# A fused retention and feed-forward kernel on one NeuronCore: FF units grouped by four for the weight loads, and alpha loaded straight into its place

## The chip, the core and the metric

The kernel runs on one core of a Trainium2 chip. The metric is the time of one execution on the device in microseconds (us), smaller being better. The times of the kernel before are 307.03, 307.56 and 306.79 us: a median of 307.03 us. The profiled execution, from which all rows of the trace come, took 306.96 us itself.

## What is computed

Two layers stand behind each other. The first is a retention layer (attention without a softmax, with a decay that depends on the distance of two positions) for 8 batches, 8 heads, 576 positions and 64 elements per head. The second is a feed-forward (FF) layer on the 4608 tokens that come out, with 512 inputs, 2048 FF units and a "snake" activation.

```python
scores = scale * (q @ k.T)                     # per batch and head
ret = scores * Dmat                            # gamma[h] ** (i - j) for i >= j, else 0
x = (ret @ v)                                  # 4608 x 512 after joining the heads
h = x @ w_in                                   # 4608 x 2048
s = sin(alpha * h)                             # alpha: one number for each FF unit
g = h + s * s / (alpha + 1e-9)
out = g @ w_out                                # 4608 x 512
```

Everything comes in and goes out as 32-bit floats (f32); the products are made from 16-bit floats (f16). The FF units may be numbered in any order inside the kernel, if the columns of w_in, the entries of alpha and the rows of w_out all follow the same order.

## The kernel before

**FF layer.** The 4608 tokens are nine blocks of 512. For a block n and a group fc of 128 FF units, `project(n, fc)` (L516) makes four matmuls at L524, one for each 128 rows of w_in: the stationary operand (the weights, loaded by a weight load of its own) is a 128 x 128 piece of w_in, the moving operand 512 token columns of `xT`. Some calls are split in two halves of 256 columns. `sine` (L529) on ScalarE makes sin(alpha h) from the PSUM result with alpha as a scale for each partition, `square` (L537) squares it on ScalarE, VectorE or GpSimd, and `product` (L546) on VectorE puts h + s s / alpha into `gT`. `gemm2(n, u)` (L562) then multiplies: 128 tokens of gT are the weights, a row group of w_out (128 x 512) the moving operand, 16 row groups summed for each 128 tokens; `finish` (L556) copies the sum to SBUF and stores it.

**Retention layer.** `load` (L110) fetches q, k and v of one batch and one half of the positions with one DMA of 512 KB on SyncE's queue; `cast` (L133) scales them to f16 on GpSimd (`G_`), VectorE (`V`) or ScalarE (`A_`); `turn` (L196) transposes them on TensorE and `take` (L209) copies the result out of PSUM (from batch 2 on, `crossed` transposes with a DMA instead). `outer`, `scores`, `masked`, `values`, `add_states` and `keep` then make the tokens' `xT`.

**Order of work.** The order is written out by hand, call after call, from L629 on: each engine executes its own calls in the order of the text. Up to L1113 the first three token blocks are interleaved with the first batches; from L1115 on a loop does the rest by a fixed plan. So an engine that waits for something holds back all that stands behind it on that engine, and TensorE's order is the same in every run.

**Loads of the weights.** w_in and w_out are loaded by GpSimd's DMA queue, which casts f32 to f16 under way, in four quarters each: `load_w_in(g)` (L90) fetches 512 columns of all four row groups, `load_w_out(g)` (L94) fetches 512 rows. In both, what is contiguous in DRAM is 512 f32, 2 KB: each DMA of 1 MB of f32 consists of 512 such runs. They stand in GpSimd's order at L656, L659, L678, L688 (w_in, quarters 0, 2, 1, 3) and L690, L727, L737, L773 (w_out, quarters 0 to 3). SyncE's queue meanwhile loads q, k and v in the order L637 to L799, among them batch 1's k for its two halves (L759, L763) and v for its second half (L799). Their consumers are the casts of k on GpSimd (L760 and L783), the turns on TensorE behind them (L764 and L800), and the cast of v on ScalarE (L807, L808) with `outer` behind it (L809).

**alpha.** alpha is loaded by ScalarE's queue as 16 partitions of 128 contiguous numbers (`alpha_r`, L631), transposed by a small matmul against a 16 x 16 identity that stands in the constants (`turn_alpha`, L582, called at L667), and copied to `alpha_t`, 128 partitions of 16 numbers (`take_alpha`, L586, L668). Column fc of `alpha_t` holds the alphas of the FF units 128 fc to 128 fc + 127.

Of the kernel before, what the change touches and what calls it, by code (L numbers as in the profile page):

```python
# [10 lines left out]
F32 = mybir.dt.float32  # L11
F16 = mybir.dt.float16
# [5 lines left out]
def kernel(  # L18
# [13 lines left out]

    nc = tc.nc

    B, H, S, D = q.shape
    DM, FF = moe_w_in.shape
    NT = out.shape[0]
    P = 128  # L40
    assert (H, S, D) == (8, 576, 64) and H * D == DM and B * S == NT
    FC = FF // P
    KT = DM // P
# [6 lines left out]
    cn_np = np.zeros((P, 84), dtype=np.float64)  # L50
# [6 lines left out]
        cn_np[:, 40 + h] = scale * gamma[h] ** (ii - 64)  # L57
    for a in range(4):
        cn_np[:, 48 + a] = gamma[4 * hi + a] ** 128
    cn_np[0:16, 68:84] = np.eye(16)  # L60

    cn_dram = nc.inline_tensor(cn_np.astype(np.float32), name="rt_cn")

    const = ctx.enter_context(tc.tile_pool(name="c", bufs=1))
    work = ctx.enter_context(tc.tile_pool(name="w", bufs=1))
    psum = ctx.enter_context(tc.tile_pool(name="p", bufs=1, space=bass.MemoryType.PSUM))
# [4 lines left out]
    cn = const.tile([P, 84], F32, tag="cn", bufs=1)  # L71
    fac = {"k": cn[:, 0:16], "q": cn[:, 16:32], "halved k": cn[:, 52:68]}
    fac_s = {"k": cn[:, 32:40], "q": cn[:, 40:48]}
    g1 = cn[:, 48:52]
    eye = cn[0:16, 68:84]
    alpha_r = const.tile([FC, P], F32, tag="alpha_r", bufs=1)
    alpha_t = const.tile([P, FC], F32, tag="alpha", bufs=1)
    inva = const.tile([P, FC], F32, tag="inva", bufs=1)
    w_in16 = const.tile([P, KT, FF], F16, tag="w_in16", bufs=1)
    w_out16 = const.tile([P, FC, 512], F16, tag="w_out16", bufs=1)  # L80
    sS = const.tile([P, B, 4, D], F16, tag="sS", bufs=1)
    xS = const.tile([P, KT, 512], F16, tag="xS", bufs=1)

    src = {"q": q, "k": k, "v": v}
    w_in_r = moe_w_in.rearrange("(a p) f -> p a f", p=P)
    w_out_r = moe_w_out.rearrange("(a p) d -> p a d", p=P)

    V, A_, G_ = nc.vector, nc.scalar, nc.gpsimd

    def load_w_in(g):  # L90
        cols = slice(g * 512, (g + 1) * 512)
        nc.gpsimd.dma_start(w_in16[:, :, cols], w_in_r[:, :, cols])  # L92

    def load_w_out(g):  # L94
        nc.gpsimd.dma_start(w_out16[:, 4 * g : 4 * g + 4, :], w_out_r[:, 4 * g : 4 * g + 4, :])

    def halves(n):
        return slice(64 * n, 64 * n + 64)
# [118 lines left out]
    matmul = nc.tensor.matmul  # L217
# [287 lines left out]
    xs = {8: xS}  # L505
    gT = {}
    hps_of = {}
# [3 lines left out]
    def bank(tag):  # L511
        if tag[0] == "m":
            return psum.tile([P, 2, 512], F32, tag=tag, bufs=1, name="hps")[:, 0]
        return psum.tile([P, 512], F32, tag=tag, bufs=1, name="hps")

    def project(n, fc, tag, part=None):  # L516

        if n not in gT:
            gT[n] = work.tile([P, FC, 512], F16, tag="gT", bufs=2, name="gT")
        if (n, fc) not in hps_of:  # L520
            hps_of[n, fc] = [bank(tag), None]
        cols = PART[part]
        for a in range(KT):
            matmul(  # L524
                hps_of[n, fc][0][:, cols], w_in16[:, a, fc * P : (fc + 1) * P], xs[n][:, a, cols],
                start=(a == 0 and part != 1), stop=(a == KT - 1), skip_group_check=True,
            )

# [46 lines left out]
    held = {}  # L575

    def keep_busy(n, tag, m=512):
        idle = psum.tile([P, 512], F32, tag=tag, bufs=1, name="idle")
        for _ in range(n):
            matmul(idle[:, 0:m], zero[:, 0:P], zero[:, 0:m], start=True, stop=True)  # L580

    def turn_alpha():  # L582
        held["al"] = psum.tile([P, FC], F32, tag="op", bufs=1, name="al_ps")
        matmul(held["al"], alpha_r, eye, start=True, stop=True, is_transpose=True)

    def take_alpha():  # L586
        nc.scalar.copy(alpha_t, held["al"])

    def invert_alpha():
        nc.vector.tensor_scalar_add(inva, alpha_t, 1e-9)  # L590
        nc.vector.reciprocal(inva, inva)
# [5 lines left out]
    def make_constants():  # L597

        ge = mybir.AluOpType.is_ge
        nc.gpsimd.memset(ident, 0.0)  # L600
        nc.gpsimd.affine_select(
            out=ident, in_=ident, compare_op=mybir.AluOpType.not_equal, fill=1.0,
            base=0, pattern=[[-1, P]], channel_multiplier=1,
        )
        nc.gpsimd.memset(mask, 1.0)
        for g in range(2):
            m = mask[halves(g), 0:256].rearrange("p (r g i) -> p r g i", r=2, g=2)
            nc.gpsimd.affine_select(
                out=m, in_=m, compare_op=ge, fill=0.0,
                base=0, pattern=[[-1, 2], [1, 2], [2, 64]], channel_multiplier=-2,  # L610
            )
            m = mask[halves(g), 256:320]
            nc.gpsimd.affine_select(
                out=m, in_=m, compare_op=ge, fill=0.0, base=0, pattern=[[1, 64]], channel_multiplier=-1,
            )
# [12 lines left out]
    with tc.manual_schedule():  # L628
        nc.scalar.dma_start(cn, cn_dram.ap())  # L629
        make_constants()  # L630
        nc.scalar.dma_start(alpha_r, moe_alpha.rearrange("(a p) -> a p", p=P))  # L631
        first = work.tile([P, 1], F32, tag="first", bufs=1, name="first")
        nc.vector.memset(first, 0.0)
        nc.scalar.activation(first, first, mybir.ActivationFunctionType.Sin)
# [19 lines left out]
        load(0, "q", 1)  # L654
        cast(0, "q", 1, G_)
        load_w_in(0)  # L656
        load(0, "k", 1)
        cast(0, "k", 1, V)
        load_w_in(2)  # L659
        turn(0, "q", 1, "h0")  # L660
        at[0].scores(0, 1, "m0")
# [2 lines left out]
        take(0, "k", 1, A_)  # L664
        load(0, "v", 1)
        at[0].scores(0, 0, "m1")
        turn_alpha()  # L667
        take_alpha()  # L668
        keep_busy(10, "h2", 256)
        take(0, "q", 1, A_)  # L670
        load(1, "q", 1)
# [4 lines left out]
        at[0].masked(0, 1)  # L676
        at[0].masked(0, 0)
        load_w_in(1)  # L678
        at[0].outer((1,), "h2", "h1")
        cast(1, "q", 1, G_)  # L680
# [7 lines left out]
        load_w_in(3)  # L688
        at[0].to_state(2, G_)
        load_w_out(0)  # L690
        at[0].values(0, False, "m0")
        at[0].values(0, True)
# [5 lines left out]
        at[0].add_states(1)  # L698
        at[0].keep(0, V)
        project(0, 2, "m1", 0)  # L700
        at[0].keep(1, V, A_)
        project(0, 2, "m1", 1)
        sine(0, 2)
        project(0, 1, "op")
        keep_busy(2, "h0")
        square(0, 2, V)
# [18 lines left out]
        product(0, 3)  # L725
        project(0, 11, "m1")
        load_w_out(1)  # L727
        sine(0, 8)
        turn(1, "q", 0, "op")
# [5 lines left out]
        square(0, 6, V)  # L735
        at[0].to_state(3, G_)
        load_w_out(2)  # L737
        square(0, 11, A_)
        product(0, 6)
# [456 lines left out]
        for c in range(3):  # L1196
            tag = next(h)
# [3 lines left out]
        for cols, eng in ((slice(0, 320), A_), (slice(320, 512), V)):  # L1201
            tag = next(h)
# [33 lines left out]
```

## Time and profile before

| what | value |
|---|---|
| time, median of 3 runs | 307.03 us (306.79 to 307.56) |
| the profiled execution's own time | 306.96 us |
| its span from the first to the last instruction | 305.2 us |
| TensorE's share of the span with a matmul under way | 96% |
| VectorE, ScalarE, GpSimd busy | 67%, 60%, 45% |
| bytes read from and written to DRAM | 36.75 MB and 9.44 MB |

The 1.8 us between the span and the time lie outside the first and the last instruction. "PE" is TensorE's matmuls, "PEld" its weight loads, "DVE" VectorE, "ACT" ScalarE, "POOL" GpSimd, "SPq" SyncE's DMA queue. A busy TensorE says only that a matmul was under way, not that it ran at its full rate. "L524" is line 524 of the kernel. In rows of instructions a number pair at the head is start and length in microseconds, "x16" is a count, and the bracket at the end is how long the engine stood idle before it and what ended the wait. In rows of DMA queues, q1 is SyncE's queue, q0 GpSimd's and q10 ScalarE's; the three numbers are packets, megabytes written, and the time that the packets took as a share of 16 DMA engines over the stretch (reads and writes overlap, so more than 100% is possible).

### The profile page before, as it was taken

To read this page: it belongs to the slowest core of one execution; us is meant where nothing else is said; L and a number is where in the kernel's file an instruction comes from. 1 tells how busy PE (TensorE), PEld (TensorE's weight loads), DVE (VectorE), ACT (ScalarE), POOL (GpSimd) and SP (SyncE) were. 2 spreads that over 40 slices of the span, in tenths; PEclk is the share of its full clock that TensorE was granted. 3 is DMA by queue.
4 is the path that set the end of the run, shared out by engine and by line. 5 is a ranking of instruction groups with operands and counts; after the bars stand their busy time and mean duration, and the time that the engine had idled before them with its cause. 6 is when DMAs were issued, how large, how long until landed. Compare 5 with 4: busy or idle time off the path is not lost.

```text
span 305.2 us, 7933 instructions
## 1 busy us (share of the span) xinstructions
PE 293.5 (96%) x3257; PEld 149.6 (49%) x3257; DVE 204.5 (67%) x296; ACT 182.7 (60%) x294; POOL 136.2 (45%) x155
## 2 busy tenths in 40 slices
PE   6879989999999999999999999999999999999995
PEld 5655556455444544454445444544454454444443
DVE  2768988899679796767665777566666746555600
ACT  1649935675365758665677567756764556555411
POOL 4794760498379488578039726653030000000000
PEclk9799999999999999999999999999999999999999
DMA  8999999997695978978689989866441111111132
GB/s 232 338 217 216 216 247 330 242 312 188 166 256 167 167 175 199 255 124 181 146 226 178 170 190 257 161 143 161 105 112 37 34 37 37 35 35 37 46 88 72
DMA packets 115508, 49.85 MB, mean 163 GB/s; under 512 B 69760, under 2 KB 110992, under 8 KB 115472
## 3 DMA queue, kind: packets, MB, share of 16 engines
q1 hardware_dynamic: 110912, 44.97, 62.8%
q0 software_dynamic: 4224, 4.19, 8.1%
q8 instruction: 25, 0.41, 0.6%
q10 hardware_dynamic: 336, 0.18, 0.3%
q14 instruction: 11, 0.09, 0.1%
HBM read 36.75 MB, written 9.44 MB: 151 GB/s over the span
## 4 chain that ended last, share of the span: by engine, by line
PE 82%; DMA 9%; POOL 3%; DVE 2%; ACT 1%; SPq 1%; issue 1%; DVEq 0%; ACTq 0%
PE ops L567 39%; PE hps L524 36%; DMA v<-in_v_dram 7%; PE sc L347 2%; PE o L389 2%; DMA q<-in_q_dram 2%; PE kv L283 1%; POOL q L169 1%; SPq L121 1%; POOL w_in L92 1%; PE o L411 1%; DVE ss_t L543 1%; DVE k L169 0%; DVE ret L359 0%; ACT v L102 0%
## 5 line engine op out<-in xcount | busy, mean ns | idle before, releaser
L567 PE MATMUL ops<-w_out,gT 128*128 128x512 f16 (+2 forms) x592 | 142.4, 373 | 0.9 <-DMA w_out<-in_moe_w_out_dram 0.4
L548 DVE SCALAR_TENSOR_TENSOR gT<-ss_t,inva,hps 128x512 f16<-128x512 f16 x144 | 106.2, 745 | 52.0 <-ACT ss_t L541 45.5
L532 ACT ACTIVATE s_t<-hps,alpha_t 128x512 f16<-128x512 f32 x144 | 97.3, 687 | 70.9 <-PE hps L524 68.1
L524 PE MATMUL hps<-xT,w_in 128*128 128x512 f16 (+1 forms) x544 | 126.5, 367 | 0.3
L524 PEld LDWEIGHTS <-w_in 128*128 128x128 f16 x608 | 58.6, 98 | 64.5 <-DVE xT L104 0.6
L567 PEld LDWEIGHTS <-gT 128*128 128x128 f16 x592 | 56.3, 98 | 65.0 <-issue 1.6
L543 DVE TENSOR_TENSOR ss_t<-s_t 128x512 f16<-128x512 f16 x72 | 43.6, 608 | 19.3 <-ACT s_t L532 18.7
L541 ACT ACTIVATE ss_t<-s_t 128x512 f16<-128x512 f16 x62 | 38.8, 632 | 0.9
L102 ACT COPY osb<-ops 128x512 f32<-128x512 f32 (+1 forms) x34 | 19.7, 582 | 22.0 <-PE ops L567 20.6
L169 POOL TENSOR_TENSOR k<-k,cn 128x1024 f16<-128x1024 f32 (+1 forms) x13 | 22.3, 1712 | 22.1 <-DMA k<-in_k_dram 17.9
L169 POOL TENSOR_TENSOR q<-q,cn 128x1024 f16<-128x1024 f32 (+1 forms) x16 | 27.2, 1710 | 10.9 <-DMA q<-in_q_dram 10.9
L359 DVE TENSOR_TENSOR ret<-sc,mask 128x1024 f16<-128x1024 f32 x20 | 23.9, 1219 | 4.2 <-PE sc L347 4.2
L329 POOL TENSOR_TENSOR kvs<-s,kvs 128x256 f32<-128x256 f32 x22 | 16.2, 734 | 4.0 <-ACT kvs L102 2.3
L543 POOL TENSOR_TENSOR ss_t<-s_t 128x512 f16<-128x512 f16 x10 | 10.8, 1084 | 14.6 <-ACT s_t L532 14.6
L102 ACT CAST xT<-o 128x1024 f16<-128x1024 f32 (+1 forms) x14 | 13.2, 957 | 6.1 <-PE o L411 5.9
L524 PE MATMUL hps<-xS,w_in 128*128 128x512 f16 x64 | 16.4, 379 | 0.0
L153 POOL TENSOR_TENSOR ks<-ks,cn 128x512 f16<-128x512 f32 x4 | 4.2, 1044 | 24.6 <-DMA vs<-in_v_dram 18.1
L104 POOL CAST v<-v 128x1024 f16<-128x1024 f32 (+1 forms) x10 | 10.0, 1007 | 11.1 <-DMA v<-in_v_dram 11.1
L328 POOL TENSOR_TENSOR s<-kvs,cn 128x256 f32<-128x256 f32 x22 | 14.3, 650 | 0.3
L321 POOL TENSOR_TENSOR s<-kvs,cn 128x256 f16<-128x256 f32 x19 | 12.2, 646 | 0.9 <-ACT kvs L102 0.4
L389 PE MATMUL o<-ret,v 64*64 64x128 f16 (+1 forms) x512 | 11.0, 214 | 0.9 <-DVE ret L359 0.4
L359 DVE TENSOR_TENSOR ret<-sc,mask_halved 128x768 f16<-128x768 f32 x12 | 11.4, 950 | 0.0
(62 smaller groups left out, 148.9 us busy)
## 6 DMA issues: line engine op xcount, KB each, us to landing
out_dram<-osb SPq DMA_DIRECT2D x70, 128.0 KB, 2.8
q<-in_q_dram SPq DMA_DIRECT2D x16, 512.0 KB, 5.4
k<-in_k_dram SPq DMA_DIRECT2D x10, 512.0 KB, 5.6
v<-in_v_dram SPq DMA_DIRECT2D x10, 512.0 KB, 6.4
k<-in_k_dram SPq DMA_DIRECT2D x24, 128.0 KB, 3.1
v<-in_v_dram SPq DMA_DIRECT2D x24, 128.0 KB, 3.3
w_in<-in_moe_w_in_dram POOLq DMA_DIRECT2D x4, 512.0 KB, 11.6
w_out<-in_moe_w_out_dram POOLq DMA_DIRECT2D x4, 512.0 KB, 11.5
```

Source lines behind the costliest of these rows:

```text
L102: eng.copy(d_, s_)
L169: eng.tensor_tensor(dst[:, a0:a1].rearrange("p a r t d -> p t (a r) d"), t_.rearrange("p (t a) x -> p t a x", t=2)[:, :, a0:a1].rearrange( ...
L328: nc.gpsimd.tensor_tensor(s32, self.kvs[:, c - 1], g1.unsqueeze(2).to_broadcast([P, 4, D]), MULT)
L329: nc.gpsimd.tensor_tensor(self.kvs[:, c], s32, self.kvs[:, c], ADD)
L359: nc.vector.tensor_tensor(ret.rearrange("p t (z x) -> p (t z) x", z=2)[:, :, 0:n], sc.rearrange("p t (z x) -> p (t z) x", z=2)[:, :, 0:n], ...
L389: made.append(matmul(o[t][halves(e), c : c + 128].rearrange("p (r i) -> p r i", r=2)[:, :, i0:64], v16[halves(g), 4 * t + 2 * x + e, r, :] ...
L524: matmul(hps_of[n, fc][0][:, cols], w_in16[:, a, fc * P : (fc + 1) * P], xs[n][:, a, cols], start=(a == 0 and part != 1), stop=(a == KT - ...
L532: nc.scalar.activation(s_t, hps, mybir.ActivationFunctionType.Sin, bias=0.0, scale=alpha_t[:, fc : fc + 1],)
L541: nc.scalar.activation(ss_t, s_t, mybir.ActivationFunctionType.Square)
L543: eng.tensor_tensor(ss_t, s_t, s_t, MULT)
L548: nc.vector.scalar_tensor_tensor(gT[n][:, fc, :], ss_t, inva[:, fc : fc + 1], hps, MULT, ADD)
L567: matmul(ops[n, c, cols.start][:, cols], gT[n][:, fk, c * P : (c + 1) * P], w_out16[:, fk, cols], start=(fk == 0), stop=(fk == FC - 1), sk ...
```

## The change

FF unit 512 g + 4 p + j now belongs to quarter g, partition p, place j. Its row of w_out goes to partition p of row group 4 g + j; so the four rows that one partition takes in a quarter lie behind one another in DRAM, one run of 8 KB, and a DMA of w_out consists of 128 runs, not 512. The columns of w_in are still loaded in their old order, in runs of 2 KB, now into four tiles, one for each quarter; `project` picks the 128 columns of a group with a step of 4 elements (8 bytes), so all weight loads at L524 read SBUF with that step. alpha is loaded directly into `alpha_t`: 128 partitions of four runs of four numbers (16 bytes) each, 512 runs; the matmul that transposed it, the copy behind it, the identity in the constants and the tile `alpha_r` are gone. The order of the instructions on each engine is the same otherwise. One wait moves: the matmul for alpha had waited for alpha's DMA, now the first `sine` and the first instruction of `invert_alpha` do.

```diff
-    alpha_r = const.tile([FC, P], F32, tag="alpha_r", bufs=1)
...
-    w_in16 = const.tile([P, KT, FF], F16, tag="w_in16", bufs=1)
+    w_in16 = [const.tile([P, KT, 512], F16, tag=f"w_in16_{g}", bufs=1, name=f"w_in16_{g}") for g in range(4)]
...
-    w_out_r = moe_w_out.rearrange("(a p) d -> p a d", p=P)
+    w_out_r = moe_w_out.rearrange("(g p j) d -> p g j d", p=P, j=4)
...
-        nc.gpsimd.dma_start(w_in16[:, :, cols], w_in_r[:, :, cols])
+        nc.gpsimd.dma_start(w_in16[g], w_in_r[:, :, cols])
...
-        nc.gpsimd.dma_start(w_out16[:, 4 * g : 4 * g + 4, :], w_out_r[:, 4 * g : 4 * g + 4, :])
+        nc.gpsimd.dma_start(w_out16[:, 4 * g : 4 * g + 4, :], w_out_r[:, g])
...
-                hps_of[n, fc][0][:, cols], w_in16[:, a, fc * P : (fc + 1) * P], xs[n][:, a, cols],
+                hps_of[n, fc][0][:, cols], w_in16[fc // 4][:, a, fc % 4 :: 4], xs[n][:, a, cols],
...
-    def turn_alpha():
-        held["al"] = psum.tile([P, FC], F32, tag="op", bufs=1, name="al_ps")
-        matmul(held["al"], alpha_r, eye, start=True, stop=True, is_transpose=True)
-
-    def take_alpha():
-        nc.scalar.copy(alpha_t, held["al"])
...
-        nc.scalar.dma_start(alpha_r, moe_alpha.rearrange("(a p) -> a p", p=P))
+        nc.scalar.dma_start(
+            alpha_t.rearrange("p (g j) -> p g j", j=4), moe_alpha.rearrange("(g p j) -> p g j", p=P, j=4)
+        )
...
-        turn_alpha()
-        take_alpha()
```

More of the change, by code (lines that the diff above doesn't have):

```diff
@@ L59 @@
         cn_np[:, 48 + a] = gamma[4 * hi + a] ** 128
-    cn_np[0:16, 68:84] = np.eye(16)
     cn_dram = nc.inline_tensor(cn_np.astype(np.float32), name="rt_cn")
@@ L74 @@
     g1 = cn[:, 48:52]
-    eye = cn[0:16, 68:84]
-    alpha_r = const.tile([FC, P], F32, tag="alpha_r", bufs=1)
     alpha_t = const.tile([P, FC], F32, tag="alpha", bufs=1)
     inva = const.tile([P, FC], F32, tag="inva", bufs=1)
-    w_in16 = const.tile([P, KT, FF], F16, tag="w_in16", bufs=1)
+    w_in16 = [const.tile([P, KT, 512], F16, tag=f"w_in16_{g}", bufs=1, name=f"w_in16_{g}") for g in range(4)]
     w_out16 = const.tile([P, FC, 512], F16, tag="w_out16", bufs=1)
```

## The prediction, as it was made before the changed kernel had run

> **What bounds the kernel now.** I read the page first (span, busy shares, chain by engine), then the chain in order of time, then the DMA queues and the engines in the stretch where the chain leaves TensorE.
>
> ```profile
> span 305.2 us, 7933 instructions
> ...
> PE 293.5 (96%) x3257; PEld 149.6 (49%) x3257; DVE 204.5 (67%) x296; ACT 182.7 (60%) x294; POOL 136.2 (45%) x155
> ...
> PE 82%; DMA 9%; POOL 3%; DVE 2%; ACT 1%; SPq 1%; issue 1%; DVEq 0%; ACTq 0%
> ```
>
> ```profile
> 3.35 5.95 DMA q<-in_q_dram
> ...
> 9.36 1.90 POOL q L169
> ...
> 11.26 1.58 POOL w_in L92 x2
> ```
>
> ```profile
> 20.57 22.89 DMA v<-in_v_dram
> ...
> 43.48 1.15 ACT v L102 x2
> ...
> 44.67 0.45 PE kv L283 x32
> ...
> 54.76 0.86 PE ops L567 x4
> 55.62 0.86 PE hps L524 x4
> ```
>
> From about 45 us TensorE is the chain: four matmuls of 512 columns take 0.86 us, 215 ns each, whether L524 or L567. Ahead of that the end hangs on loads: q's second half releases GpSimd at 9.36, which then issues w_in, and batch 1's second v, issued at 20.57, is consumed only at 43.48. So there are two questions: does the change make TensorE's steady 215 ns longer, and does it move the loads before 45 us? A TensorE delay at 45 us stays to the end, since its order is fixed and from there it hardly waits.
>
> Why the loads are late shows in the DMA queues over three stretches: 3 to 12 us, 16 to 40 us, and all up to 30.4 us.
>
> ```profile
> q1 hardware_dynamic: 6151, 3.10, 114.2%
> ```
>
> ```profile
> q0 software_dynamic: 3428, 3.41, 83.6%
> q1 hardware_dynamic: 3443, 1.74, 35.4%
> ```
>
> ```profile
> q1 hardware_dynamic: 10424, 5.26, 63.2%
> q0 software_dynamic: 2268, 2.26, 43.7%
> ```
>
> Alone, q1 (runs of 512 bytes) moves 6151 packets in 9 us: 9000 x 16 / 6151 = 23.4 ns a packet and engine. Beside q0 (2 KB read, 1 KB written as f16) the two queues move **one packet each in turn**: 3428 against 3443 in 24 us, 112 ns a pair, so 88.6 ns for a packet of q0. Per byte read both cost the same (21.9 and 23.1 bytes per ns): the engines are full and bound by bytes.
>
> **Step 1, w_out in runs of 8 KB.** Each DMA has 128 packets of 8192 / 23.1 = 354 ns instead of 512 of 88.6 ns; from the two sizes seen, hardly a nanosecond is saved by fewer packets. But if a turn stays one packet, q1 gets one packet in 378 ns instead of in 112 ns while w_out streams. [...]
>
> Who is waiting on q1 then? A load of 512 KB is 1024 packets and 16 that signal, 1040; one of the weights 512 and 16, 528. At 30.4 us q0 has moved four quarters of w_in (2112) and 156 packets of w_out; at 143 a microsecond (24 us for 3428) w_out began at 29.3. q1 had then moved 10424 - 156 = 10268, so batch 1's first k, the tenth load (10400 in all), lacked 132: 8.25 an engine. Before, that is over at 30.2; after, 8.25 x 378 ns = 3.1 us, so 32.4. Here are its consumers, on GpSimd and TensorE, and the count of q1 at 38.3 us:
>
> ```profile
> 31.39 2.07 POOL L169 TENSOR_TENSOR k<-k,cn 128x1024 f16<-128x1024 f32 x1
> 33.42 1.04 POOL L543 TENSOR_TENSOR ss_t<-s_t 128x512 f16<-128x512 f16 x1
> 36.43 1.04 POOL L543 TENSOR_TENSOR ss_t<-s_t 128x512 f16<-128x512 f16 x1 [1.98 <-ACT s_t L532]
> 37.41 0.80 POOL L95 DMA_DIRECT2D w_out<-in_moe_w_out_dram  x1
> 38.59 1.89 POOL L169 TENSOR_TENSOR k<-k,cn 128x1024 f16<-128x1024 f32 x1 [0.38 <-DMA k<-in_k_dram]
> ```
>
> ```profile
> 33.52 0.62 PE L202 MATMUL tr<-ident,k 128*128 128x128 f16 x8
> ...
> 38.10 1.02 PE L567 MATMUL ops<-w_out,gT 128*128 128x512 f16 x4 [0.42 <-DMA w_out<-in_moe_w_out_dram]
> ...
> 41.96 0.61 PE L202 MATMUL tr<-ident,k 128*128 128x128 f16 x8
> ...
> 44.67 0.45 PE L283 MATMUL kv<-v,k 64*64 64x64 f16 x32 [0.67 <-ACT v L102]
> ```
>
> ```profile
> q1 hardware_dynamic: 11560, 5.83, 57.5%
> ```
>
> The second k (11440 packets) is complete on average 120 packets before 38.3, at 37.5; its cast starts at 38.59. So a cast starts 1.1 us after the average engine is done. The first k's cast moves to 32.4 + 1.1 = 33.5, ends 2.07 later at 35.6, and the transposes behind it, which ran at 33.52 with no slack, start 2.05 us later: **+2.05**. Behind them on TensorE the wait for w_out at 38.10 goes (its second quarter lands after 16 turns of 378 ns, at 35.4): **-0.42**. The second k: three quarters of w_out are 24 turns, to 29.3 + 9.1 = 38.4; q1 is then at 10268 + 384, and the missing 788 packets take 49 x 23.4 ns = 1.15 us: 39.5, cast 40.6 to 42.5. TensorE reaches its transposes at 41.96 + 2.05 - 0.42 = 43.6, so that is hidden. Batch 1's second v, the twelfth load, follows 1.5 us after k, at 41.0. Counts up to 41.9 us, and of q0 up to 43.0 us:
>
> ```profile
> q1 hardware_dynamic: 12941, 6.53, 58.6%
> q0 software_dynamic: 3696, 3.67, 51.6%
> ```
>
> ```profile
> q0 software_dynamic: 3832, 3.81, 52.2%
> ```
>
> Before, q1 was 461 packets past v's 12480 at 41.9, so v was complete at 41.2, 2.3 us ahead of its cast. At 41.0 the cast is ready in time, and TensorE's wait of 0.67 at 44.67 is swallowed: **-0.67**. Sum of the step: +0.96.
>
> One thing decides whether that holds: the last quarter of w_out. 3696 is exactly seven quarters, and 136 packets by 43.0 put the eighth's start at 42.05, 4.6 us after its issue at 37.41. The square ahead of it waits for TensorE's work behind the transposes, so its issue moves to 39.5, and with the same 4.6 us it starts at 44.1, after v. That nearest row is what I take; if a quarter of the runs makes the start quicker than 1.5 us, it comes ahead of v (rival 1). GpSimd's 0.80 for each w_out issue may shrink to nothing; nothing on the path is behind it (a cast whose transposes are not late, squares that wait for ScalarE), so 0. w_in's runs in DRAM stay 2 KB, so its four tiles cost and save nothing.
>
> **Step 2, weights read with a step of 8 bytes.** No row shows such a load. A packed one is here:
>
> ```profile
> L524 PEld LDWEIGHTS <-w_in 128*128 128x128 f16 x608 | 58.6, 98 | 64.5 <-DVE xT L104 0.6 <-issue 0.5 <-DMA w_in<-in_moe_w_in_dram 0.4
> ```
>
> It takes 98 ns beside a matmul of 215 ns, so it may more than double at no cost to 544 of the 608; to the 64 with 256 columns (half of 215, 108 ns) only 10 ns are free. Lower end: 0, or a little below if nothing else moves. Upper end, if a load fetches four elements for each it uses: 392 ns, 544 x 177 + 64 x 284 = 114 us. The nearest row is the packed load, so I take 0. [...]
>
> **Step 3, alpha.** The small matmul and copy go; what stands behind them is this, on TensorE and on ScalarE:
>
> ```profile
> 13.82 0.23 PE L584 MATMUL al_ps<-cn,alpha_r 16*128 16x16 f32 x1
> ...
> 17.48 0.62 PE L202 MATMUL tr<-ident,q 128*128 128x128 f16 x8 [1.43 <-POOL q L169]
> ```
>
> ```profile
> 14.49 0.18 ACT L587 COPY alpha_t<-al_ps 128x16 f32<-128x16 f32 x1
> ...
> 18.14 1.01 ACT L102 COPY qT<-tr 128x1024 f16<-128x1024 f16 x1 [1.34 <-PE tr L202]
> ```
>
> Both engines wait for GpSimd by 17.48 anyway: gain 0. The load gets 512 packets of 16 bytes, 32 an engine where there was one, while q1 is full. Price of a small packet: q1 in 62.8 to 64.2 us, where its runs have 256 bytes:
>
> ```profile
> q1 hardware_dynamic: 1577, 0.40, 130.8%
> ```
>
> 1400 x 16 / 1577 = 14.2 ns. 32 of them are 0.45 us; at the 23.4 ns of 512 bytes 0.75; on the line through the two sizes (5.3 ns at 16 bytes) 0.17. I take the nearest row, less the one packet that goes: **+0.43** on q's landing before 9.36, which is on the chain, and on all loads behind. The new wait for alpha costs nothing: its old load landed 3.7 us after it was issued in the first microseconds, and the first sine is much later:
>
> ```profile
> alpha_r<-in_moe_alpha_dram ACTq DMA_DIRECT2D x1, 8.0 KB, 3.7
> ```
>
> ```profile
> 22.30 1.49 ACT L532 ACTIVATE s_t<-hps,alpha_t 128x512 f16<-128x512 f32 x2 [0.82 <-PE hps L524]
> ```
>
> **Sum.** 2.05 - 0.42 - 0.67 + 0.43 = +1.39 on the profiled 306.96 (its span of 305.2 and 1.8 around it; the median is 307.03): **308.3 us**.
>
> **Rivals.**
> 1. *The last quarter of w_out comes early* and eight turns of 354 ns (2.8 us) fall ahead of v. v is complete at 43.8; with the 1.1 us above and the cast's 1.15, TensorE's `outer` starts at 46.1, with the 2.3 us that v's cast had after v's average at 47.2: +1.4 to +2.5, with alpha 308.8 to 309.9, middle 309.4. Ahead of k as well: cast 43.4 to 45.3, transposes 3.3 later, less 0.67, with alpha 310.1. For it: fewer runs to write out. Against: the 4.6 us above.
> 2. *The change does not coarsen the turns*: the queue cuts a run into pieces, or a turn holds several short packets already. Then only alpha is left, 307.1 to 307.4. [...] The one-to-one count speaks against.
> 3. *Weight loads with a step become the bound*, from 108 ns on for the halves and from 215 ns for the rest. At twice 98 ns: 64 x 88 = +5.6 us, 314; at four times 421. For: the fetched bytes. Against: 118 ns of room.
> 4. *Faster*: turns by bytes, and an 8 KB packet cheaper than four. From 45 ns less of 354 on (24 packets ahead of v save 1.09 us), both TensorE waits, 0.42 and 0.67, go without a stall in their place; with alpha's runs free 306.96 - 1.09 = 305.9. For: a waiting DMA ends both waits. Against: equal cost per byte at 512 bytes and 2 KB.
>
> **How the numbers follow.** Forecast 0.35, rival 1 0.26, rival 2 0.21, rival 3 0.10, rival 4 0.08. The forecast's own stretch is 307.5 to 309.1 (alpha 0.17 to 0.75, half a microsecond on the first k). 0.3% is 0.92 us, about what a measurement of this kernel can tell from no change. Slower: 0.27 of the forecast's 0.35, all of rivals 1 and 3: 0.63. Same: the rest of the forecast and rival 2: 0.29. Faster: 0.08. The range leaves out rival 3 and most of rival 4: 306.7 to 310.6.
>
> **What would show it.** Right: q0 at about a quarter of its packets for w_out, q1 near 42 packets a microsecond from 30 to 38 us; GpSimd's cast of the first k near 33.5 with a DMA wait ahead of it and TensorE's transposes idle for 2 us at 33.5; no wait for w_out at 38; then 0.86 us for four matmuls as before. Wrong: unchanged counts (rival 2), a later v (rival 1), loads at L524 well over 98 ns (rival 3). A fall of the granted clock after the new stall would add to it, and is not in the sum.

## The result, and the profile after

The changed kernel takes **310.42 us** in the median of 20 runs (306.72 to 314.95); the kernel before, on the same chips, 306.80 us (20 runs, 305.62 to 307.60). The ratio to before is 1.0046, with a 95% interval of 1.0028 to 1.0065. Runs over 1.5% above a kernel's fastest are left out of that ratio, here ten of the twenty, the profiled one (313.22 us) among them; the experiments show that it is the change that makes them, so the median of all, 3.6 us above before's, stands beside it. The twenty spread over 8 us, where before's stay within 2: the size of the loss differs from run to run, and why it does is the main question below.

The page of after, the rows that answer to those of before (span, busy shares, the chain by engine, the weight loads of `project`). Lines stand one lower than before here: L523 is the former L524.

```profile
span 311.5 us, 7929 instructions
...
PE 297.6 (96%) x3256; PEld 160.5 (52%) x3256; DVE 204.7 (66%) x296; ACT 183.1 (59%) x293; POOL 136.1 (44%) x155
...
PE 90%; issue 2%; DMA 2%; POOL 2%; DVE 1%; ACT 1%; SPq 1%; DVEq 0%; ACTq 0%; POOLq 0%
...
L523 PEld LDWEIGHTS <-w_in 128*128 128x128 f16 x608 | 68.4, 115 | 58.6 <-issue 2.3
```

The span is 6.3 us longer, yet TensorE is busy 4.1 us more. So a part of the loss is idle time and a part is matmuls that last longer. The weight loads with a step take 115 ns, not 98. Where the time goes is read in TensorE's order around the first k of batch 1:

```profile
27.70 6.27 PE L523 MATMUL hps<-xT,w_in 128*128 128x512 f16 x32
38.74 1.03 PE L201 MATMUL tr<-ident,k 128*128 128x128 f16 x8 [4.76 <-POOL k L168]
39.57 5.09 PE L523 MATMUL hps<-xT,w_in 128*128 128x512 f16 x16
...
51.09 0.42 PE L282 MATMUL kv<-v,k 64*64 64x64 f16 x32
```

Before, the transposes stood at 33.52 with no wait; now they wait 4.76 us for GpSimd. The 16 matmuls behind them take 5.09 us; before it was 2.85:

```profile
33.98 2.85 PE L524 MATMUL hps<-xT,w_in 128*128 128x512 f16 x16
```

The waits for w_out at 38.10 and for v at 44.67 are gone: neither `outer` at 51.09 nor the eight matmuls with w_out at 44.49 have a bracket. `outer` comes 6.42 us later than before's 44.67, and the end 6.3 us. So everything is decided by 51 us. GpSimd names the cause, and the stretches of the engines (the number behind the busy times is the granted clock, 1.00 being full) show what came with it:

```profile
36.78 1.90 POOL L168 TENSOR_TENSOR k<-k,cn 128x1024 f16<-128x1024 f32 x1 [4.90 <-DMA k<-in_k_dram]
```

```profile
33.50:37.40 3.90, 0.48 (x5) 0.21 (x2) 1.39 (x2) 0.96 (x2) 0.62 (x1) 1.00 1.06 217
37.50:44.20 6.70, 5.46 (x23) 3.12 (x24) 3.57 (x6) 3.17 (x5) 4.01 (x5) 0.50 1.05 304
44.30:48.00 3.70, 3.45 (x77) 1.89 (x76) 1.96 (x3) 1.95 (x5) 2.04 (x2) 1.00 1.12 292
```

The cast waits for the k itself, and behind the idle stretch TensorE's clock is granted at half for 6.8 us. The DMA queues from 30 to 38 us, before and then after:

```profile
q0 software_dynamic: 1153, 1.14, 84.1%
q1 hardware_dynamic: 1154, 0.58, 35.3%
```

```profile
q0 software_dynamic: 388, 1.37, 84.6%
q1 hardware_dynamic: 866, 0.44, 21.6%
```

GpSimd's queue moves a third of the packets and more bytes in the same time, and SyncE's queue loses 288 packets.

A quicker run of the same kernel (307.55 us) was profiled too. TensorE, GpSimd and ScalarE there:

```profile
35.74 0.62 PE L201 MATMUL tr<-ident,k 128*128 128x128 f16 x8 [1.58 <-POOL k L168]
36.20 2.76 PE L523 MATMUL hps<-xT,w_in 128*128 128x512 f16 x16
...
43.52 0.61 PE L201 MATMUL tr<-ident,k 128*128 128x128 f16 x8
...
45.39 0.42 PE L282 MATMUL kv<-v,k 64*64 64x64 f16 x32
```

```profile
33.78 1.90 POOL L168 TENSOR_TENSOR k<-k,cn 128x1024 f16<-128x1024 f32 x1 [2.05 <-DMA k<-in_k_dram]
...
39.64 0.59 POOL L94 DMA_DIRECT2D w_out<-in_moe_w_out_dram  x1
40.59 1.89 POOL L168 TENSOR_TENSOR k<-k,cn 128x1024 f16<-128x1024 f32 x1 [0.36 <-DMA k<-in_k_dram]
```

Here the stall is 1.58 us, the clock stays full (2.76 us for the 16 matmuls), and `outer` is 0.72 us later than before. So one kernel has two courses, and both lose at the same instruction.

### The profile page after: what moved, and what is told of

Same layout as the page of the kernel before. It is cut to its first block, busy times and chain, and to the rows that moved or that the text cites. A ratio compares the mean times of both kernels' runs of the same rounds, so it can differ in the third digit from the quotient of the medians.

```text
span 311.5 us, 7929 instructions
## 1 busy us (share of the span) xinstructions
PE 297.6 (96%) x3256; PEld 160.5 (52%) x3256; DVE 204.7 (66%) x296; ACT 183.1 (59%) x293; POOL 136.1 (44%) x155
## 4 chain that ended last, share of the span: by engine, by line
PE 90%; issue 2%; DMA 2%; POOL 2%; DVE 1%; ACT 1%; SPq 1%; DVEq 0%; ACTq 0%; POOLq 0%
PE ops L566 40%; PE hps L523 39%; PE sc L346 3%; PE o L388 2%; DMA q<-in_q_dram 2%; PE kv L282 2%; PE tr L201 1%; PE idle L579 1%; SPq L120 1%; PE o L410 1%; DVE ret L358 1%; ACT s_t L531 1%; POOL q L168 1%; POOL k L168 1%; DVE xT L103 0%
## 5 line engine op out<-in xcount | busy, mean ns | idle before, releaser
L523 PE MATMUL hps<-xT,w_in 128*128 128x512 f16 (+1 forms) x544 | 129.0, 372 | 0.2 <-DVE xT L103 0.2
L523 PEld LDWEIGHTS <-w_in 128*128 128x128 f16 x608 | 68.4, 115 | 58.6 <-issue 2.3
L542 DVE TENSOR_TENSOR ss_t<-s_t 128x512 f16<-128x512 f16 x72 | 40.4, 562 | 19.3 <-ACT s_t L531 18.7
L168 POOL TENSOR_TENSOR k<-k,cn 128x1024 f16<-128x1024 f32 (+1 forms) x13 | 21.5, 1653 | 28.4 <-DMA k<-in_k_dram 23.4
L523 PE MATMUL hps<-xS,w_in 128*128 128x512 f16 x64 | 16.4, 379 | 0.0
L103 POOL CAST v<-v 128x1024 f16<-128x1024 f32 (+1 forms) x10 | 11.0, 1112 | 5.2 <-DMA v<-in_v_dram 5.2
```

Source lines behind the costliest of these rows:

```text
L168: eng.tensor_tensor(dst[:, a0:a1].rearrange("p a r t d -> p t (a r) d"), t_.rearrange("p (t a) x -> p t a x", t=2)[:, :, a0:a1].rearrange( ...
L523: matmul(hps_of[n, fc][0][:, cols], w_in16[fc // 4][:, a, fc % 4 :: 4], xs[n][:, a, cols], start=(a == 0 and part != 1), stop=(a == KT - 1 ...
L542: eng.tensor_tensor(ss_t, s_t, s_t, MULT)
```

## The experiments

**Theory.** A turn of GpSimd's queue lasts as long as one packet (before moved 1153 of its packets beside 1154 of SyncE's from 30 to 38 us), so runs of 8 KB hold back the first k of batch 1, which SyncE's queue loads at the same time; the other two parts of the change are free. **Rivals**: the weight loads with a step or alpha's short runs carry the loss; long runs cost by themselves, wherever they stand; the long stall has a cause of its own.

| kernel | runs | median, us | all runs, us | ratio to before, 95% interval |
|---|---|---|---|---|
| E1, before with w_out's long runs alone | 12 | 311.4 | 306.96 to 314.69 | 1.0053 (1.0022 to 1.0084) |
| E2, before with alpha alone | 12 | 306.68 | 306.15 to 307.98 | 1.0004 (0.9987 to 1.0021) |
| E3, before with the step alone | 12 | 306.83 | 305.79 to 307.77 | 0.9995 (0.9979 to 1.0010) |
| E4, after with w_out in 2 KB pieces | 12 | 306.86 | 306.38 to 307.60 | 1.0003 (0.9990 to 1.0016) |
| E5, after with 4 KB pieces | 8 | 307.92 | 306.90 to 310.14 | 1.0044 (1.0021 to 1.0067) |
| E6, after with 1 KB pieces | 4 | 309.92 | 309.81 to 310.10 | 1.0102 (1.0087 to 1.0116) |
| E7, after with TensorE kept busy | 5 | 311.89 | 311.33 to 313.49 | 1.0181 (1.0160 to 1.0203) |
| E8, after again | 8 | 309.90 | 306.88 to 313.56 | 1.0057 (1.0030 to 1.0083) |
| E9, after, long runs in quarter 3 only | 12 | 309.08 | 306.94 to 311.80 | 1.0060 (1.0029 to 1.0091) |
| E10, after with k ahead of v | 12 | 306.66 | 306.09 to 307.39 | 0.9992 (0.9979 to 1.0006) |
| E11, before with k ahead of v | 12 | 307.26 | 306.39 to 307.79 | 1.0011 (0.9996 to 1.0026) |
| E12, after with quarters 1 and 2 issued later | 11 | 307.25 | 306.70 to 308.26 | 1.0009 (0.9999 to 1.0020) |

Before, run beside them, had medians from 306.77 to 306.90 us and no run over 307.9. The ratios are made like that of the result.

### E1, E2 and E3: each part alone

E1, the part that concerns w_out:

```diff
-    w_out_r = moe_w_out.rearrange("(a p) d -> p a d", p=P)
+    w_out_r = moe_w_out.rearrange("(g p j) d -> p g j d", p=P, j=4)
...
-        nc.gpsimd.dma_start(w_out16[:, 4 * g : 4 * g + 4, :], w_out_r[:, 4 * g : 4 * g + 4, :])
+        nc.gpsimd.dma_start(w_out16[:, 4 * g : 4 * g + 4, :], w_out_r[:, g])
```

> The kernel before with one part alone: the rows of w_out are grouped into runs of 8 KB, while w_in and alpha stay as before (so units and rows no longer belong together; the work is the same). Theory (turns of the queues): q0 moves 128 packets for a quarter of w_out, q1 falls to about 42 packets a microsecond while they stream, GpSimd's cast of batch 1's first k starts 2 us later or more, TensorE stands still ahead of the transposes behind it for 2 to 5 us, and where that stall is long the granted clock halves for a while: 308 to 314 us, in two groups as the changed kernel. Rival (alpha's small runs at the start put SyncE's queue behind and make the stall): within 0.3% of before.

TensorE's and GpSimd's rows of its profile (313.62 us):

```profile
39.50 1.03 PE L202 MATMUL tr<-ident,k 128*128 128x128 f16 x8 [5.43 <-POOL k L169]
```

```profile
37.54 1.90 POOL L169 TENSOR_TENSOR k<-k,cn 128x1024 f16<-128x1024 f32 x1 [5.52 <-DMA k<-in_k_dram]
```

The same stall, the same spread up to 314.7: this part alone makes the loss.

E2, alpha alone:

```diff
-        nc.scalar.dma_start(alpha_r, moe_alpha.rearrange("(a p) -> a p", p=P))
+        nc.scalar.dma_start(
+            alpha_t.rearrange("p (g j) -> p g j", j=4), moe_alpha.rearrange("(g p j) -> p g j", p=P, j=4)
+        )
...
-        turn_alpha()
-        take_alpha()
```

> The kernel before with alpha alone changed: loaded in place in 512 runs of 16 bytes, without the matmul and the copy (the entries then belong to other units than w_in's columns; the work is the same). Theory: all loads land 0.2 to 0.45 us later, and nothing else: +0.2 to +0.5 us, within 0.3%. Rival (alpha's runs delay SyncE's queue so that batch 1's loads fall behind w_in): a stall ahead of the transposes at 33.5 us, and 308 us or more.

```profile
9.70 1.90 POOL L169 TENSOR_TENSOR q<-q,cn 128x1024 f16<-128x1024 f32 x1 [3.59 <-DMA q<-in_q_dram]
```

GpSimd's wait for q is 3.59 us here and 3.52 to 3.59 in the ten profiles with the short runs; in the four without, before among them, it is 3.39 to 3.42. So the short runs do cost about 0.16 us on this load. At the end nothing of it is to be seen (0.13% less to 0.21% more).

E3, the step alone:

```diff
-                hps_of[n, fc][0][:, cols], w_in16[:, a, fc * P : (fc + 1) * P], xs[n][:, a, cols],
+                hps_of[n, fc][0][:, cols], w_in16[fc // 4][:, a, fc % 4 :: 4], xs[n][:, a, cols],
```

> The kernel before with the weight loads of w_in alone changed: four tiles and a step of 4 elements (the columns then belong to other units than alpha and w_out have; the work is the same). Theory: the loads take 113 ns in place of 98 as in the changed kernel, hidden beside 215 ns of matmul, and at most 64 x 5 ns are seen: 0 to +0.3 us. Rival (a longer load costs at each of the 608 matmuls): 608 x 15 ns = +9 us, or a part of it.

Its groups of instructions, the weight loads:

```profile
L524 PEld LDWEIGHTS <-w_in 128*128 128x128 f16 x608 | 67.7, 114 | 57.8 <-DMA w_in<-in_moe_w_in_dram 1.3 <-issue 0.6 <-DVE xT L104 0.4
```

Each load takes 16 ns more, and the time stays: they run beside matmuls of 215 ns, and even the 64 beside matmuls of 108 ns show nothing at the end.

### E4, E5 and E6: the size of the pieces

All three are after with one argument more, which cuts the same runs into smaller pieces (2048, 4096, 1024 bytes):

```diff
-        nc.gpsimd.dma_start(w_out16[:, 4 * g : 4 * g + 4, :], w_out_r[:, g])
+        nc.gpsimd.dma_start(w_out16[:, 4 * g : 4 * g + 4, :], w_out_r[:, g], max_dma_last_dim=2048)
```

> The changed kernel with one part undone: w_out is cut into pieces of 2 KB again (512 packets for a quarter), all else as changed. Theory (turns): counts of q0 and q1 stay one to one at 112 ns a pair, the stall at 33.5 us is gone or under 0.5 us, the time is that of before plus alpha's 0.2 to 0.5 us: 307.0 to 307.4, in one group. Rival (alpha or the step make the loss): stays at 308 to 314 us.

TensorE with 2 KB pieces:

```profile
34.00 0.62 PE L201 MATMUL tr<-ident,k 128*128 128x128 f16 x8
...
38.57 1.02 PE L566 MATMUL ops<-w_out,gT 128*128 128x512 f16 x4 [0.42 <-DMA w_out<-in_moe_w_out_dram]
...
44.89 0.44 PE L282 MATMUL kv<-v,k 64*64 64x64 f16 x32 [0.42 <-ACT v L101]
```

No stall at the transposes, the waits for w_out and v are back, and the time is that of before, a little under the 307.0 to 307.4 expected, since nothing of alpha's term shows. The numbering of the units is still the new one: it is the length of a turn that costs.

> The changed kernel with w_out cut into pieces of 4 KB (256 packets for a quarter). Theory (length of a turn): one packet of q0 in about 200 ns instead of 378 or 112, q1 at about 80 packets a microsecond; the wait ahead of the cast of batch 1's first k is between those of 2 KB and 8 KB, TensorE's stall behind it 0.3 to 2 us: 306.9 to 308.5 us, and no run above 311. Rival (only the grouping into one run counts, or the stall has another cause): two groups up to 314 as with 8 KB.

With 4 KB pieces GpSimd's cast of k starts at 34.31 us, and TensorE waits 2.34 us:

```profile
36.27 0.62 PE L201 MATMUL tr<-ident,k 128*128 128x128 f16 x8 [2.34 <-POOL k L168]
```

The loss lies between that of 2 and of 8 KB, as a cost per turn would have it. Two of the eight runs (309.14 and 310.14) lie over the 308.5 expected.

> The changed kernel with w_out cut into pieces of 1 KB (1024 packets for a quarter), so shorter turns than before. Theory (turns): one to one again, about 68 ns a pair; batch 1's k and v land earlier, w_out later: TensorE waits 1 to 2.5 us for w_out's second quarter near 38 us where it waited 0.42, and its wait for v goes: 307 to 308.3 us, with no stall ahead of the transposes of k. Rival (more packets cost nothing and give q1 its share): 306.5 us or less.

This one came out slower than expected. The k is in time, but now w_out itself is late:

```profile
34.08 0.62 PE L201 MATMUL tr<-ident,k 128*128 128x128 f16 x8
...
40.93 1.86 PE L566 MATMUL ops<-w_out,gT 128*128 128x512 f16 x4 [2.76 <-DMA w_out<-in_moe_w_out_dram]
```

Twice the turns, each still shared one for one with SyncE's queue (1695 packets of q0 and 1696 of q1 from 30 to 38 us), make w_out the late load; the clock falls to half for 3.4 us at the end of that wait (1.86 us for four matmuls). So 2 KB lies between two losses here: pieces of 1 KB starve w_out (2.76 us), pieces of 4 KB k (2.34).

### E7: the stall filled with matmuls

```diff
+        keep_busy(24, "h2")
         turn(1, "k", 0, "op")
```

> The changed kernel with 24 idle matmuls of 512 columns (24 x 215 ns = 5.2 us) put ahead of the transposes of batch 1's first k, where TensorE stalls. They can't make it faster than its own quick runs; they fill the longest stall seen. Theory (in the long runs the stall lets the granted clock halve for two periods of 3.4 us, and that makes a part of their loss): the clock stays full after 34 us, the two groups become one at 306.96 + 5.2 - 0.42 - 0.67 = about 311 us, no run above 312. Rival (the long runs are long for another reason): runs at 313 to 315 remain, or 316 and more where the loss adds to the 5.2.

```profile
34.19 5.34 PE L579 MATMUL idle<-zero 128*128 128x512 f16 x24 [0.27 <-DVE gT L547]
39.37 0.61 PE L201 MATMUL tr<-ident,k 128*128 128x128 f16 x8
39.81 2.76 PE L523 MATMUL hps<-xT,w_in 128*128 128x512 f16 x16
...
49.01 0.42 PE L282 MATMUL kv<-v,k 64*64 64x64 f16 x32
```

The 24 matmuls last as long as the long wait in every run, so all five runs pay it. The clock stays full (granted 1.00 from 33 to 52 us): from the transposes to `outer` 9.64 us, as in the quicker run of after (45.39 - 35.74 = 9.65), where the profiled run of after took 51.09 - 38.74 = 12.35. The halved clock is thus worth 2.7 us, and with the idle stretch filled it does not come. Two of the runs lie over the 312 expected. In the profiled one (313.06) `outer` is 4.34 us later than before and the end 6.1; between 110 and 150 us TensorE waits 1.4 us for nothing that the trace names, which is most of the difference. The other (313.49) has no profile, and neither is followed further.

Behind the filling, the load of k takes the long course here too, as GpSimd's cast shows:

```profile
37.34 1.90 POOL L168 TENSOR_TENSOR k<-k,cn 128x1024 f16<-128x1024 f32 x1 [5.46 <-DMA k<-in_k_dram]
```

### E8: the changed kernel again

> The changed kernel once more, for a profile of one of its quick runs if one comes. Theory: where q1 had no hole of more than 1 us at 15 to 17 us, batch 1's first k lands 2 to 4 us earlier than in the profile of 313.2 us, TensorE's stall at 34 us is 1 to 2.5 us, and the time 307 to 309 us; where the hole is there, the stall is 4 us or more and the time over 311 us. Rival: the hole and the stall have nothing to do with one another.

Again some runs near 307 (306.88 to 307.77), two at 309.9 and some over 312 (312.63 to 313.56). Its profiled run is the quicker one shown above. The two profiles of the same kernel differ long before the k: SyncE's queue at 15 to 17 us, in the long run first, then in the quick one.

```profile
q1 hardware_dynamic: 155, 0.07, 13.4%
```

```profile
q1 hardware_dynamic: 280, 0.14, 29.6%
```

And the sums up to 29.3 us, when w_out begins, in the same order:

```profile
q1 hardware_dynamic: 10064, 5.08, 62.3%
q0 software_dynamic: 2105, 2.16, 43.2%
```

```profile
q1 hardware_dynamic: 10228, 5.16, 63.8%
q0 software_dynamic: 2053, 2.06, 41.3%
```

The long run has a **gap** in SyncE's queue and starts into w_out about 160 packets behind. The gap isn't made by the change: of the other profiles, E1, E2, E5, E6, E7, E10 and E11 have it (82 to 147 packets from 15 to 17 us), and before, E3, E4, E8, E9 and E12 don't (201 to 280). What it leaves behind is alike in all: when w_out begins, 316 to 381 packets of SyncE's first ten loads are lacking in the eight profiles with the gap, and 108 to 131 in the six without. With turns of 2 KB it does no harm: E2 has it, its transposes wait 0.75 us, and the waits behind swallow that (its `outer` starts at 44.63, before's at 44.67).

Why does a gap of some ten packets an engine cost 3 us more? The cast waits for the last of the 16 DMA engines' signals: in the long run it starts at 36.78, behind the last signal at 36.40, and in the other four profiles below 0.36 to 0.43 us behind theirs (before 31.39 and 30.96, E8 33.78 and 33.41, E1 37.54 and 37.18, E7 37.34 and 36.94). The times of these signals (DMA packets of 4 bytes, by their ends) in the trace, for the first k of batch 1 and for the first quarter of w_out:

| profile | k, by engine | w_out's quarter 0, by engine |
|---|---|---|
| before | 13 at 29.67 to 30.36, 3 at 30.75 to 30.96 | 13 at 32.33 to 33.03, 3 at 33.71 to 34.03 |
| after, quick run (E8) | 15 at 30.52 to 32.38, 1 at 33.41 | 13 at 31.92 to 32.32, 3 at 33.39 to 33.76 |
| after, long run | 14 at 31.59 to 33.03, **2 at 36.36 and 36.40** | 13 at 31.26 to 32.07, 3 at 32.93 to 33.36 |
| E1 | 14 at 31.54 to 32.78, **2 at 37.17 and 37.18** | 13 at 31.20 to 31.80, 3 at 32.38 to 33.45 |
| E7 | 13 at 31.65 to 33.04, **3 at 34.64, 36.03 and 36.94** | 13 at 31.34 to 32.25, 3 at 32.48 to 33.41 |

The last three engines end quarter 0 behind the other thirteen in every profile, by 0.2 to 1.9 us. How long a turn is shows in the same signals: where quarter follows on quarter, one engine ends them 2.75 us apart (32.93 and 35.68 on a late engine of the long run), 8 turns of 344 ns. In the long run (10400 - 10071) / 16 = 21 packets of k were lacking on each engine when w_out began (10071 is the sum above and the 7 packets until w_in's 2112 of q0 are over). Quarter 0 covers about 9 turns, its signal's among them. The 12 left over run at 23.4 ns each, 0.3 us, wherever q0 pauses between two quarters. From 31.5 to 32.25 us most engines have that pause:

```profile
q1 hardware_dynamic: 319, 0.16, 72.1%
q0 software_dynamic: 23, 0.06, 38.2%
```

On the late two quarter 1 stands already behind quarter 0 when that ends at 32.9, and ten more turns of 344 ns lead to 36.4. (The trace does not number the engines; that the late signals of k and of quarter 0 belong to the same engines is inferred from these distances.) In the quick run (10400 - 10287) / 16 = 7 packets were lacking (10228 and 59 more until w_in is over), fewer than the 8 turns of quarter 0, so no engine gets into quarter 1. E12 tests this.

### E9: long runs for the last quarter only

```diff
-        nc.gpsimd.dma_start(w_out16[:, 4 * g : 4 * g + 4, :], w_out_r[:, g])
+        nc.gpsimd.dma_start(w_out16[:, 4 * g : 4 * g + 4, :], w_out_r[:, g], max_dma_last_dim=8192 if g == 3 else 2048)
```

> The kernel after with 8 KB runs for the last quarter of w_out only; quarters 0 to 2 are cut into pieces of 2 KB. Theory (a long turn costs only while a load with a near consumer is queued in SyncE's queue beside it): the last quarter moves after 44 us, when batch 1's loads are in, so no stall ahead of the transposes of the first k, no halved clock after it: 306.8, within 0.4, and no run over 308. Rival (8 KB runs cost by themselves, wherever they stand): about a quarter of the loss of w_out alone, 307.8 or more.

The expectation failed, by more than the rival's number; only four of the twelve runs stay near 307 (306.94 to 307.24). TensorE and ScalarE:

```profile
46.56 0.45 PE L282 MATMUL kv<-v,k 64*64 64x64 f16 x32 [2.33 <-ACT v L101]
46.94 3.50 PE L566 MATMUL ops<-w_out,gT 128*128 128x512 f16 x8
```

```profile
45.37 1.14 ACT L101 CAST v<-v 128x512 f16<-128x512 f32 x2 [4.16 <-DMA v<-in_v_dram]
```

But the long quarter doesn't cost by itself: it is batch 1's second v that is held back. Its signals came at 40.99 to 41.34 from 13 engines, and at 44.33, 44.92 and 45.04 from the late three. I had put the quarter after 44 us; without a stall ahead of it GpSimd issues it at 37.79 and it starts near 42, just in time to catch the late engines. In after its issue stands at 43.33, behind v; in E8 it stands at 39.64, and its first packet starts at 41.55, when v's last signal comes. So the theory stands, and "where nothing urgent is queued" has to be looked up, not assumed.

### E10 and E11: k ahead of v in SyncE's queue

```diff
+        load(1, "k", 0)
         load(1, "v", 0)
...
-        cast(1, "v", 0, A_)
...
-        load(1, "k", 0)
...
         sine(0, 10)
+        cast(1, "v", 0, A_)
```

> The kernel after with batch 1's first k loaded ahead of batch 1's first v (two issues of SyncE's queue change places), and that v's cast moved on ScalarE behind the sine of group 10, where v is late enough. All 8 KB runs stay. Theory (the loss is this one k, queued beside long turns): the first k is complete before w_out starts, its cast runs as before or earlier, no stall at the transposes and no halved clock; the second k's transposes may now wait up to 1 us, since no earlier stall swallows it, and the wait of 0.42 for w_out is gone: 306.9 (306.4 to 307.7), in one group, no run over 309. Rival (long turns slow all that is queued, so another load takes the place of k): a stall of 2 us or more elsewhere, 308.5 or more, and runs over 311 again.

GpSimd and TensorE in E10:

```profile
31.69 2.08 POOL L168 TENSOR_TENSOR k<-k,cn 128x1024 f16<-128x1024 f32 x1
```

```profile
33.82 0.62 PE L201 MATMUL tr<-ident,k 128*128 128x128 f16 x8
34.28 2.76 PE L523 MATMUL hps<-xT,w_in 128*128 128x512 f16 x16
...
44.14 0.42 PE L282 MATMUL kv<-v,k 64*64 64x64 f16 x32
```

All long runs are in, the profiled run has the gap (105 packets), and the whole loss is gone, the upper group of runs with it. The load that now stands in k's place, batch 1's first v, ends at 36.38 on its last engine, as k did, and nobody waits: ScalarE casts it at 36.70. Neither of before's two waits is left. So long runs don't cost by themselves either.

> The control of the one above: the kernel before with the same change of places and the same move of the cast. The theory expects nothing: the first k's transposes had no wait, and the waits for w_out (0.42) and v (0.67) stay: 306.8 within 0.4. If it is faster or slower by over 0.9, the move has an effect of its own, to be taken off from the run above.

E11's `outer` waits longer for v, not shorter, and its time is that of before within the interval (0.04% less to 0.26% more):

```profile
45.84 0.45 PE L283 MATMUL kv<-v,k 64*64 64x64 f16 x32 [1.40 <-ACT v L102]
```

So the move has no gain of its own that E10 could owe its time to.

### E12: the second quarter issued later

```diff
-        load_w_out(1)
...
-        load_w_out(2)
...
         square(0, 7, G_)
+        load_w_out(1)
+        load_w_out(2)
```

> The kernel after with the issues of w_out's quarters 1 and 2 moved on GpSimd behind the square of group 7, some 3 us later (both still ahead of the cast of batch 1's first k); all 8 KB runs stay. In the profile of after, 14 of the 16 engines end this k at 31.6 to 33.0 us, between quarter 0 and quarter 1, and two lagging engines at 36.4, since quarter 0 ends on them at 32.9 to 33.4, when quarter 1 already stands behind it. Theory (the long stall is two late engines caught by the second long quarter): with quarter 1 issued near 32 and starting near 36, the late engines end k within half a microsecond of quarter 0's end, at 33.9 at the latest; cast at 34, transposes near 36, a stall of about 2 us whether or not the load is behind, no halved clock after it: 307.7 (307.0 to 308.9) in one group, no run over 310; a wait of up to 0.7 for w_out may come. Rival (the backlog alone sets the stall, with or without quarter 1): k still at 36, and half the runs over 311. Second rival: quarter 1 is now late itself, with a wait of 2 us or more for w_out at the second group of four matmuls, 309 or more in all runs.

```profile
31.56 1.14 POOL L94 DMA_DIRECT2D w_out<-in_moe_w_out_dram  x2
33.47 1.90 POOL L168 TENSOR_TENSOR k<-k,cn 128x1024 f16<-128x1024 f32 x1 [0.77 <-DMA k<-in_k_dram]
```

```profile
35.42 0.62 PE L201 MATMUL tr<-ident,k 128*128 128x128 f16 x8 [1.37 <-POOL k L168]
```

One group of runs, none over 308.26, and no wait for w_out behind it. A pause between the two quarters takes the long stall away in all eleven runs. The profiled run has no gap (265 packets), so that the late engines finish early with a gap too is argued from the eleven times, not seen. Since eight of the fourteen profiles have the gap, eleven runs without one would be a rare chance.

## Why the prediction held, and where its sizes were off

The forecast was 308.3 us, slower, with 306.7 to 310.6 around it; the median is 310.42. Its mechanism is what the runs show, and the term that was mis-sized is the +2.05. Ten of the twenty runs lie above the range, so that the median stays inside it, by 0.18 us, is luck in part.

- **Step 1, the turns.** One packet each in turn: held at each length counted (pieces of 1 KB, 1695 packets of q0 and 1696 of q1 in E6; 2 KB, 1153 and 1154 before; 8 KB, 107 and 109 from 32 to 34 us in E8). A turn of 8 KB is 344 ns, not 378. One sign named for this step did not come: from 30 to 38 us q1 moved 108 packets a microsecond in the long run (866 in all, 319 of them in the 0.75 us from 31.5, when most engines had nothing of q0) and 78 in E8 (623), not 42.
- **Step 1, the first k: +2.05.** In the quick course the transposes came 2.22 us later than before (35.74 against 33.52), 1.58 of it the stall, with the cast at 33.78 where 33.5 was forecast, the second k's cast at 40.59 (40.6), and its transposes at 43.52 (43.6). In the long course they came 5.22 us later, with a stall of 4.76 (E1: 5.43), and there the sum failed. It took the average engine and 1.1 us for the last one, a distance seen with turns of 112 ns. On average k was complete even in the long run at 32.0 us (10402 packets); the last engine came 4.4 us later. The signals above lie far apart (3.3 us between the fourteenth and the fifteenth), and the cast started only behind the last one (36.40 and 36.78); the sum should have been made with that one.
- **Step 1, the waits for w_out (-0.42) and v (-0.67).** Both are gone in both profiles: held. From the transposes to `outer` E8 takes 9.65 us and before took 11.15, which is 1.50 less where 1.09 was summed.
- **The clock.** It was named as what would add and is not in the sum. It fell in the long course and cost 2.7 us (E7).
- **The last quarter behind v.** It held, but not by the 4.6 us between issue and start: in E8 1.9 us lie between the issue at 39.64 and the first packet at 41.55, and v was complete at 41.55 too. That is no margin at all, so this step held by luck. Rival 1 did not happen in these profiles; E9 shows what it costs when it does: a wait of 2.33 us, with one halved period of the clock behind it.
- **Step 2, 0.** Held (E3), with 16 ns more for each load, well below the 118 ns of room. So the load is not quite at the packed one's 98 ns (114 in E3), but what is missing stays hidden. Rival 3 falls.
- **Step 3, +0.43.** The short runs cost 0.16 us on q's load, near the lower of the two bounds (its line through the two sizes gives 5.6 ns and 0.18, not 5.3 and 0.17), and nothing at the end (E2): behind it stand the waits of 0.42 and 0.67, which can swallow a shift of that size. So 14.2 ns was the wrong neighbour for a packet of 16 bytes.
- **Rivals 2 and 4** fall with the counts: the turns did become coarser. The other half of rival 4 was right in its direction: an 8 KB packet takes 344 - 23.4 = 321 ns, 33 less than the 354 of four, where it needed 45.

The two errors of size went opposite ways: alpha came out smaller, and in the long course the stall of k is larger by 2.7 and the clock costs another 2.7. The sum was thus near to the quick half only (its ten runs have a median of 308.24, though the one profiled run of the quick course, 307.55, lies 0.6 above before and not the 1.39 summed); for the other half the prediction had no number, only its last sentence.

What stays **open**: why SyncE's queue has the gap in some runs. In the profiles that have it, SyncE's load issued at about 11 us took 2.04 us or more to issue, 1.35 in the others; what makes the issue longer no run tells. That the gap decides between the two courses rests on the profiles (E1, E7 and after with it, E8 without) and on E10 and E12, which take the long stall away; the gap itself was not switched on or off. And six of the twenty runs lie between 308 and 309.5 us, and two of E8's at 309.9: none of these has a profile, so which of the terms they pay is not known.

## What to carry to other kernels

Longer runs in GpSimd's queue lengthened its turn here, for SyncE's queue on the same engines, from 114 ns (2 KB) to 344 ns (8 KB); before runs are made longer, look for the load with the nearest consumer that is still queued beside it, and count with the slowest engine, not the average. If such a load is there, bring it forward in its queue (E10) or leave a pause between the long transfers (E12) rather than give up the long runs. What the long runs win themselves was small here, 25.3 bytes read per ns and engine against 22.5.

## What the runs showed of the hardware

- **Sixteen engines, not one.** The slowest three end the first quarter of w_out 0.2 to 1.9 us behind the others in each of the fourteen profiles. In the long run of after 3.3 us lie between the fourteenth and the fifteenth engine of one load.
- **The clock changed in steps of 3.41 us.** In after it is full until 37.46 and half until 44.29, two such periods. A wait of 2.33 us in E9 and one of 2.76 in E6 halved it for one period; one of 2.34 in E5 did not. What differs is how the wait lies to the period's edges (counted on from the last change): idle for 68% of one period in E9 (44.23 to 46.56 in the one that ends at 47.07), 64% in E6, but 54% in E5, 1.86 us of the one that ends at 35.79. The periods of all fourteen profiles, counted in the same way, agree: 32 periods at full clock were idle for 56% or more, and each was followed by half; 1179 were idle for 54% or less, and none was. The full clock came back behind busier periods: 18 halved periods idle for up to 17% were followed by full, 8 idle for 17 to 44% by another halved one, as in after, where the first of the two was idle for 37%.
- **Weights with a step of 8 bytes** loaded in 114 ns instead of 98 (E3).
- **Per byte, long runs were a little cheaper.** A turn of 8 KB beside one packet of 512 bytes is 8704 bytes in 344 ns, 25.3 a ns; a quarter of 2 KB runs takes 3.65 us for 32 turns (29.05 to 32.70 on one engine of before), 2560 bytes in 114 ns, 22.5. The forecast had them equal.
